# The second product of a two-layer product in threes: each output's three matmuls one after the other

## The chip, the cores and the metric

The kernel runs on one core of a Trainium2 chip. The metric is device time in microseconds of one execution; for the kernel before there are three runs and, apart from them, one execution under the hardware profiler, which gives the profile and the trace.

## What is computed

The reference first mixes a sequence in the frequency domain, then sends every token through two layers:

```python
X = np.fft.rfft(x, axis=1)                       # x: 8 x 3008 x 256
Yr = Xr @ w_r - Xi @ w_i + b_r
Yi = Xr @ w_i + Xi @ w_r + b_i
Yr = np.sign(Yr) * np.maximum(np.abs(Yr) - 0.01, 0.0)   # Yi in the same way
y = np.fft.irfft(Y, n=3008, axis=1)
h = np.maximum(y @ w_in, 0.0)                    # 24064 tokens, 256 -> 2048
out = (h * h) @ w_out                            # 2048 -> 256
```

## The kernel before

Matmuls with fp32 accuracy are made of three: an operand is split into a high part, its cast to F32R, and a low part, what the cast left of it. A product is then high x high + high x low + low x high, added up in PSUM. `mm3` (lines 179 to 184) issues these three for one output, one after the other: line 182 takes the first stationary part with the first moving part, line 183 the same stationary part with the second moving part, line 184 the second stationary part with the first moving part.

The transform is done in stages: A (a transform of 47 points, `plan_a`, tiles xin, f, fh, fl, psa), B (a transform of 64 points, the mix with the weights, the threshold and the way back, `plan_b`, tiles bin, psb, x, xh, xl, psm, e, z, zh, zl, psc) and D (the last transform back, `plan_d`, tiles din, psd, dv, dx). The stages hand over through scratch tensors in DRAM; all DMAs are issued by SyncE (SP). D writes the high and low parts xt of the token features for chunks of 512 tokens; there are 47 chunks.

The two layers run in rounds, eight per chunk, 376 in all and three more to empty the pipeline. In round r, TensorE (PE) does the following in this order, written out by hand at the end of the kernel:

- the first product of round r (`mm1`): 12 matmuls of 512 columns into ph, two banks of PSUM with no second buffer;
- what the plan puts at "p1": a stage's matmuls (psa, psb or psd);
- the block of the second product of round k = r - 3 (`mm2`): 21 matmuls of 256 columns into four banks po0 to po3, which collect over the eight rounds of a chunk;
- what the plan puts at "p2" (psm, psc, psa or psd).

The second product is a 2 x 2 scheme with seven products instead of eight: `PLACES` names for each of the seven the half of a bank that collects it, two in each of po0, po1 and po2 and one in po3. Its weights wo are the stationary operand and lie ready in a high part `wo_[0]` and a low part `wo_[1]`; its moving operand is the hidden layer, with high part gh and low part gl.

The other engines follow in each round. ScalarE (ACT): two times ReLU out of ph (line 876), the square (line 877), what the plan has at "e", then gh for round r - 1 (line 931), what the plan has at "f" and "a". VectorE (DVE): the sums that make the seven operands (lines 882 to 884), what the plan has at "e2", then gl for round r - 1 (line 936), and what the plan has at "f2" (the bias, lines 233 and 234, which reads psm) and "v". In the last round of a chunk `put_together` (lines 898 to 912) reads the four banks: one operation of ScalarE (line 902), seven of VectorE (lines 903 to 909); gh then comes after line 902, and gl after the seven and after "f" and "f2".

gh and gl have two buffers each. gh of round r - 1 is made in round r and read by the block of round r + 2. In round r its buffer was last in use by round r - 3, whose block runs in that same round r. So gh is written when the block of the same round has finished reading the buffer. Two more buffers matter: psa, psb, psd, psm and psc share two banks (`ps_f`), so that the next of them is written when VectorE or ScalarE has read the one before the last; and the banks po0 to po3 are single.

The block of the second product, before, first goes over the seven places with both weights and gh (line 891, 14 matmuls) and then over the seven places with the high weights and gl (line 895, 7 matmuls).

Of the kernel before, what the change touches and what calls it, by code (L numbers as in the profile page):

```python
# [130 lines left out]
PLACES = ((0, 0, 0), (2, 0, 1), (6, 1, 0), (5, 1, 1), (4, 2, 0), (3, 2, 1), (1, 3, 0))  # L131
NPR = 7
NU = NF // 2
# [3 lines left out]
HALF = CH // 2  # L137
# [12 lines left out]
def fft_mix_moe(ctx: ExitStack, tc: tile.TileContext, xp, xu, w_r, w_i, b_r, b_i,  # L150
                w_in, w_out, t_u, t_a, t_b, t_b0, t_m, t_d, sgn, outT):
    nc = tc.nc
# [19 lines left out]
    wo_ = [], []  # L172
# [6 lines left out]
    def mm3(out, lt, rt, start, stop, **kw):  # L179

        (l0, l1), (r0, r1) = lt, rt
        nc.tensor.matmul(out, l0, r0, start=start, stop=False, **kw)  # L182
        nc.tensor.matmul(out, l0, r1, start=False, stop=False, **kw)  # L183
        nc.tensor.matmul(out, l1, r0, start=False, stop=stop, **kw)  # L184
# [701 lines left out]
    def mm2(j, po, gh, gl):  # L886

        for s, bank, half in PLACES:
            out = po[bank][:, half * HALF:half * HALF + HALF]
            for k in range(2):  # L890
                nc.tensor.matmul(out, wo_[k][j][:, s], gh[:, s], start=j == 0 and half == 0 and k == 0,  # L891
                                 stop=False, skip_group_check=True)
        for s, bank, half in PLACES:
            out = po[bank][:, half * HALF:half * HALF + HALF]
            nc.tensor.matmul(out, wo_[0][j][:, s], gl[:, s], start=False, stop=j == NU - 1,  # L895
                             skip_group_check=True)

    def put_together(c, po):
        p = {s: po[bank][:, half * HALF:half * HALF + HALF] for s, bank, half in PLACES}
# [15 lines left out]
    with tc.manual_schedule():  # L915
        for r in range(last + LAG):
            c, j = divmod(r, NU)
# [6 lines left out]
            k = r - LAG  # L924
# [15 lines left out]
            if k >= 0:  # L940
                if jj == 0:
                    pos[cc] = [ps_o.tile([P, 512], F32, tag=f"o{i}", name=f"po{i}") for i in range(4)]
                mm2(jj, pos[cc], *split_.pop(k))
# [54 lines left out]
```

## Time and profile before

| | |
|---|---|
| three runs, us | 2605.96, 2604.91, 2600.55 (median 2604.91) |
| the profiled execution, us | 2602.41 |
| its span, us | 2600.6 |
| granted TensorE clock, mean | 0.992 |
| matmuls | 16496 |
| of them the second product | 5264 at line 891, 2632 at line 895 |
| gh (L931), count and mean ns | 376, 1697 |
| gl (L936), count and mean ns | 376, 2022 |

The span goes from the first to the last instruction. In the rows below, a group is one line of the program on one engine with its tiles: out<-in, shapes, count, then busy time in us and the mean of one in ns, then the idle time of the engine before it and what ended most of that. PEld is TensorE's loading of weights, which runs beside its matmuls (PE). A wait names who waited, for whom, how long in total, how often, and the longest. In the timeline a row has its start, its length, engine, line and operation; rows of equal instructions are merged, with their count. The chain is the work that ended last, followed back from the end.

### The profile page before, as it was taken

What the parts mean: (1) busy time and instruction counts of PE and PEld (TensorE: products, weight loads), DVE (VectorE), ACT (ScalarE), POOL (GpSimd) and SP (SyncE); (2) the same over time, 40 slices, a digit from 0 to 9 for tenths busy, and PEclk for the clock granted to TensorE, in tenths of its full rate; (3) what the DMA queues carried; (4) which work ended last, traced back from release to release, by engine and by line L of the source; (5) the groups of instructions that cost most, each with busy time, mean ns of one, the idle gap of its engine ahead of it and who ended that gap; (6) DMA issues with size and microseconds to landing.
All of it is one profiled execution on the core that took longest, in us unless ns stands there. A gap on an engine that the chain in (4) does not pass through costs nothing.

```text
span 2600.6 us, 41936 instructions
## 1 busy us (share of the span) xinstructions
PE 2540.9 (98%) x16496; PEld 2281.6 (88%) x16496; DVE 2106.6 (81%) x3155; ACT 1993.3 (77%) x2764; POOL 48.1 (2%) x57
## 2 busy tenths in 40 slices
PE   6979999999999999999999999999999999999999
PEld 3569999999999898999889998899989898999988
DVE  5868888888888888888888888788887888777776
ACT  3668887788788787778877887778777777777776
POOL 1410000000000000000000000000000000000000
PEclk8999999999999999999999999999999999999999
DMA  8621121212221112111122112121121111100000
GB/s 254 184 85 55 52 74 61 78 60 63 77 67 55 54 56 76 59 53 52 58 78 63 53 55 68 57 69 58 44 73 52 41 37 57 36 28 28 20 24 17
DMA packets 113094, 164.59 MB, mean 63 GB/s; under 512 B 9584, under 2 KB 63074, under 8 KB 112706
## 3 DMA queue, kind: packets, MB, share of 16 engines
q1 hardware_dynamic: 112898, 161.91, 19.8%
q8 instruction: 131, 2.15, 0.3%
q14 instruction: 65, 0.53, 0.1%
HBM read 86.90 MB, written 74.97 MB: 62 GB/s over the span
## 4 chain that ended last, share of the span: by engine, by line
PE 84%; DVE 7%; ACT 5%; DMA 2%; issue 1%; SPq 0%; DVEq 0%; ACTq 0%
PE po L891 21%; PE ph L182 12%; PE ph L184 12%; PE ph L183 12%; PE po L895 10%; PE psd L268 3%; PE psb L219 3%; PE psm L182 2%; PE psm L184 2%; PE psm L183 2%; DVE gl L936 2%; ACT g L876 1%; ACT g L877 1%; DMA din<-s 1%; DVE g L882 1%
## 5 line engine op out<-in xcount | busy, mean ns | idle before, releaser
L936 DVE TENSOR_TENSOR gl<-g,gh 128x1792 fp32r<-128x1792 f32 x376 | 760.3, 2022 | 32.2 <-ACT gh L931 23.2
L876 ACT ACTIVATE g<-ph 128x512 f32<-128x512 f32 x752 | 409.1, 596 | 458.0 <-PE ph L184 456.5
L891 PE MATMUL po<-gh,wo 128*128 128x256 f32 x5264 | 695.2, 282 | 1.6 <-DVE o L908 0.8
L891 PEld LDWEIGHTS po<-gh,wo 128*128 128x128 f32 x5264 | 651.8, 188 | 15.5 <-DVE o L908 4.6
L931 ACT CAST gh<-g 128x1792 fp32r<-128x1792 f32 x376 | 638.2, 1697 | 17.2 <-PE po L891 13.6
L182 PE MATMUL ph<-xt,wi 128*128 128x512 f32 x1504 | 593.1, 394 | 11.1 <-DVE dx L276 8.5
L184 PE MATMUL ph<-xt,wi 128*128 128x512 f32 x1504 | 590.8, 393 | 0.0
L183 PE MATMUL ph<-xt,wi 128*128 128x512 f32 x1504 | 589.3, 392 | 0.0
L882 DVE TENSOR_TENSOR g<-g 128x512 f32<-128x512 f32 x376 | 259.9, 691 | 330.5 <-ACT g L877 328.6
L877 ACT ACTIVATE g<-g 128x1024 f32<-128x1024 f32 x376 | 399.6, 1063 | 12.0
L895 PE MATMUL po<-gl,wo 128*128 128x256 f32 x2632 | 368.1, 279 | 0.0
L184 PEld LDWEIGHTS ph<-xt,wi 128*128 128x128 f32 x1504 | 282.9, 188 | 65.0
L182 PEld LDWEIGHTS ph<-xt,wi 128*128 128x128 f32 x1504 | 283.1, 188 | 63.6 <-ACT xt L280 8.7
L895 PEld LDWEIGHTS po<-gl,wo 128*128 128x128 f32 x2632 | 334.5, 188 | 0.0
L183 PEld LDWEIGHTS ph<-xt,wi 128*128 128x128 f32 x1504 | 283.2, 188 | 51.7
L884 DVE TENSOR_TENSOR g<-g 128x256 f32<-128x256 f32 x376 | 159.9, 425 | 12.9
L883 DVE TENSOR_TENSOR g<-g 128x256 f32<-128x256 f32 x376 | 159.8, 425 | 12.8
L182 PE MATMUL psm<-wm,xh 128*128 128x256 f32 (+1 forms) x552 | 163.1, 295 | 3.7 <-DVE dx L276 3.1
L184 PE MATMUL psm<-wm,xl 128*128 128x256 f32 (+1 forms) x552 | 161.2, 292 | 0.0
L183 PE MATMUL psm<-wm,xh 128*128 128x256 f32 (+1 forms) x552 | 160.6, 291 | 0.0
L219 PEld LDWEIGHTS psb<-tB,bin 128*128 128x128 f32 x768 | 101.1, 194 | 35.4 <-issue 17.4
L268 PEld LDWEIGHTS psd<-tD,din 120*128 120x128 f32 (+1 forms) x832 | 107.6, 191 | 18.1 <-DMA din<-s 7.2
(102 smaller groups left out, 2569.2 us busy)
## 6 DMA issues: line engine op xcount, KB each, us to landing
bin<-s SPq DMA_DIRECT2D x96, 256.0 KB
s<-evc SPq DMA_DIRECT2D x96, 256.0 KB
outT_dram<-o SPq DMA_DIRECT2D x94, 256.0 KB
din<-s SPq DMA_DIRECT2D x96, 240.0 KB
xin<-in_xp_dram SPq DMA_DIRECT2D x72, 240.0 KB
s<-eva SPq DMA_DIRECT2D x72, 240.0 KB
s<-eva SPq DMA_DIRECT2D x22, 192.0 KB
w<-in_moe_w_in_dram SPq DMA_DIRECT2D x8, 512.0 KB
```

The source lines that it names most:

```text
L182: nc.tensor.matmul(out, l0, r0, start=start, stop=False, **kw)
L183: nc.tensor.matmul(out, l0, r1, start=False, stop=False, **kw)
L184: nc.tensor.matmul(out, l1, r0, start=False, stop=stop, **kw)
L219: nc.tensor.matmul(ps[:, k, :, q, :], tv[:, q, k], tB[:, 0:r + 2:r + 1], start=True, stop=True)
L268: nc.tensor.matmul(ps[:, k, part], t[:n, s:s + P], tD[:n, tab + part, :n], start=True, stop=True)
L876: nc.scalar.activation(g[:, 2 * a:2 * a + 2], ph[:, a].rearrange("p (t m) -> p t m", t=2), AF.Relu)
L877: nc.scalar.activation(g[:, 0:4], g[:, 0:4], AF.Square)
L882: nc.vector.tensor_sub(g[:, 4:6], g[:, 1:4:2], g[:, 0:2])
L891: nc.tensor.matmul(out, wo_[k][j][:, s], gh[:, s], start=j == 0 and half == 0 and k == 0, stop=False, skip_group_check=True)
L895: nc.tensor.matmul(out, wo_[0][j][:, s], gl[:, s], start=False, stop=j == NU - 1, skip_group_check=True)
L931: nc.scalar.copy(split_[r - 1][0], hid[r - 1])
L936: nc.vector.tensor_sub(gl, hid.pop(r - 1), gh.bitcast(F32))
```

## The change

`mm2` issues the three matmuls of each place one after the other, by `mm3`, as the first product and the stages do already. The order of the places, the number of matmuls, their operands, the banks and the number of buffers of gh and gl stay as they are. `mm3` is given the high and low weights as its two stationary parts and gh and gl as its two moving parts; so the three are: high weights with gh, high weights with gl, low weights with gh.

```diff
     def mm2(j, po, gh, gl):
 
         for s, bank, half in PLACES:
-            out = po[bank][:, half * HALF:half * HALF + HALF]
-            for k in range(2):
-                nc.tensor.matmul(out, wo_[k][j][:, s], gh[:, s], start=j == 0 and half == 0 and k == 0,
-                                 stop=False, skip_group_check=True)
-        for s, bank, half in PLACES:
-            out = po[bank][:, half * HALF:half * HALF + HALF]
-            nc.tensor.matmul(out, wo_[0][j][:, s], gl[:, s], start=False, stop=j == NU - 1,
-                             skip_group_check=True)
+            mm3(po[bank][:, half * HALF:half * HALF + HALF], (wo_[0][j][:, s], wo_[1][j][:, s]),
+                (gh[:, s], gl[:, s]), j == 0 and half == 0, j == NU - 1, skip_group_check=True)
```

The lines behind it move up by six: gh is line 925 now, gl line 930, and `put_together`'s operations are lines 896 to 903.

## Prediction

> **What bounds the kernel now.** I read the page's busy times and its chain that ended last, then the main stretch alone, then the costliest groups and the waits, and last the timeline and the chain where a wait stands.
>
> ```profile
> span 2600.6 us, 41936 instructions
> PE 2540.9 (98%) x16496; PEld 2281.6 (88%) x16496; DVE 2106.6 (81%) x3155; ACT 1993.3 (77%) x2764; POOL 48.1 (2%) x57
> ...
> PE 84%; DVE 7%; ACT 5%; DMA 2%; issue 1%; SPq 0%; DVEq 0%; ACTq 0%
> ```
>
> TensorE is the bound: 98% busy, 84% of the chain. The same by stretch, for the rounds of the main loop (columns: stretch, its length, then busy time and instructions of PE, PEld, DVE, ACT, POOL, granted clock, DMA share, GB/s):
>
> ```profile
> 165.00:2595.00 2430.00, 2414.98 (x16040) 2202.66 (x16039) 2000.11 (x2981) 1908.13 (x2611) 0.00 (x0) 1.00 0.17 54
> ```
>
> PE stands for only 2430.00 - 2414.98 = 15 us of it, at a granted clock of 1.00. So no wait that goes can give much; the change gains only if matmuls come closer together, and loses wherever it makes PE wait. The groups of the second product, and the weight loads of one third of the first (which is in threes already):
>
> ```profile
> L891 PE MATMUL po<-gh,wo 128*128 128x256 f32 x5264 | 695.2, 282 | 1.6 <-DVE o L908 0.8
> ...
> L895 PE MATMUL po<-gl,wo 128*128 128x256 f32 x2632 | 368.1, 279 | 0.0
> ...
> L183 PEld LDWEIGHTS ph<-xt,wi 128*128 128x128 f32 x1504 | 283.2, 188 | 51.7
> ```
>
> And the waits of the main stretch (total, times, longest):
>
> ```profile
> ACT g L876 <- PE ph L184: 452.1, 264, 4.6
> ...
> ACT gh L931 <- PE po L891: 13.6, 21, 1.3
> ...
> PEld psb L219 <- DVE e L233: 10.5, 14, 1.2
> ...
> PE psb L219 <- DVE e L233: 5.3, 10, 0.8
> ...
> PEld po L891 <- DVE o L908: 4.6, 16, 0.5
> ```
>
> ScalarE mostly waits for PE (452 us before L876), but in 376 - 264 = 112 rounds it does not: there it has no slack. PE's own waits are for VectorE's read of the mix (L233), which frees the bank that the next psb writes.
>
> **The order of the matmuls.** PE, the end of the second product's block before a psc (po0 to po3 the four banks, gh and gl high and low operand, wo03 and wo13 high and low weights of one j). Before:
>
> ```order
> L891 MATMUL po2_12280<-gh_12348,wo13_909 128x256
> L891 MATMUL po3_12281<-gh_12348,wo03_908 128x256
> L891 MATMUL po3_12281<-gh_12348,wo13_909 128x256
> L895 MATMUL po0_12278<-gl_12349,wo03_908 128x256 x2
> L895 MATMUL po1_12279<-gl_12349,wo03_908 128x256 x2
> L895 MATMUL po2_12280<-gl_12349,wo03_908 128x256 x2
> L895 MATMUL po3_12281<-gl_12349,wo03_908 128x256
> L182 MATMUL psc_12511<-zh_12379,tMs_63 128x512
> ```
>
> The same place now:
>
> ```order
> L183 MATMUL po2_12280<-gl_12349,wo03_908 128x256
> L184 MATMUL po2_12280<-gh_12348,wo13_909 128x256
> L182 MATMUL po3_12281<-gh_12348,wo03_908 128x256
> L183 MATMUL po3_12281<-gl_12349,wo03_908 128x256
> L184 MATMUL po3_12281<-gh_12348,wo13_909 128x256
> L182 MATMUL psc_12511<-zh_12379,tMs_63 128x512
> ```
>
> The last reader of gh was the 14th of 21 matmuls and is now the 21st. The number of matmuls and loads is the same. What this costs in three places:
>
> **1. gh's buffer comes free seven matmuls later.** gh has two buffers and is written (L931) in the round in which the block that read the same buffer two rounds back runs. ScalarE is in order: what stands behind L931 waits with it. A place without slack, in the timeline, with the same place at its last occurrence behind it, and ScalarE's busy time between:
>
> ```profile
> 830.65 0.98 PE L895 MATMUL po<-gl,wo 128*128 128x256 f32 x7
> ...
> 830.87 1.70 ACT L931 CAST gh<-g 128x1792 fp32r<-128x1792 f32 x1
> ...
> 832.16 0.39 PE L182 MATMUL ph<-xt,wi 128*128 128x512 f32 x1
> ...
> 834.90 1.80 PE L891 MATMUL po<-gh,wo 128*128 128x256 f32 x14
> ...
> 836.09 1.08 ACT L876 ACTIVATE g<-ph 128x512 f32<-128x512 f32 x2
> ...
> 837.35 0.39 PE L182 MATMUL ph<-xt,wi 128*128 128x512 f32 x1
> ...
> 1922.67 1.08 ACT L876 ACTIVATE g<-ph 128x512 f32<-128x512 f32 x2
> ...
> 1923.93 0.39 PE L182 MATMUL ph<-xt,wi 128*128 128x512 f32 x1
> ```
>
> ```profile
> 830.90:837.10 6.20, 6.20 (x41) 5.59 (x40) 5.10 (x7) 6.15 (x11) 0.00 (x0) 1.00 0.27 85
> ```
>
> gh starts at 830.87, but the block ends at 830.65 + 0.98 = 831.63: gh moves by 0.76 and the hand-over, 0.8 us. ScalarE is busy for 6.15 of the 6.20 us that follow (evc, xh, four writes of z, fh), so L876 ends at 836.09 + 1.08 + 0.8 = 837.97. The next first product, which needs the banks that L876 empties, started at 837.35; it will wait some 0.6 us. I count 9 such places in the timeline, the first and last of them quoted: 9 x 0.6 = 5.5 us. Nothing waited there before.
>
> The other kind is on the chain already (start, length, piece; the first and the last of ten, one in full; then the block it should have waited for, from the timeline):
>
> ```profile
> 747.79 1.59 ACT gh L931
> ...
> 1232.15 1.70 ACT gh L931
> ...
> 1238.47 1.07 ACT g L877
> ...
> 1239.57 0.70 DVE g L882
> ...
> 1251.00 0.61 DVE e L233
> 1251.65 1.16 PE psb L219 x8
> ...
> 2190.51 1.70 ACT gh L931
> ```
>
> ```profile
> 1231.93 0.98 PE L895 MATMUL po<-gl,wo 128*128 128x256 f32 x7
> ```
>
> From gh at 1232.15 ScalarE, then VectorE carry the chain without a pause for 19 us, across a chunk's end with its eight operations, up to psb. The block ends at 1232.91: again 0.8 us, of which some 0.1 is lost in small gaps of the chain. 10 x 0.7 = 7 us. The rows behind gh on VectorE at that place, before:
>
> ```order
> L882 TENSOR_TENSOR g_12842<-g_12842 128x512 [waits Activation_49]
> L883 TENSOR_TENSOR g_12842<-g_12842 128x256 [waits DVE_49]
> L884 TENSOR_TENSOR g_12842<-g_12842 128x256 [waits DVE_49]
> L936 TENSOR_TENSOR gl_12857<-g_12765,gh_12856 128x1792 [waits PE_49,Activation_49]
> L233 TENSOR_TENSOR e_12908<-psm1_12884,bias2_68 128x512 [waits PE_49]
> ```
>
> and now (same order):
>
> ```order
> L882 TENSOR_TENSOR g_12842<-g_12842 128x512 [waits Activation_49]
> L883 TENSOR_TENSOR g_12842<-g_12842 128x256 [waits DVE_49]
> L884 TENSOR_TENSOR g_12842<-g_12842 128x256 [waits DVE_49]
> L930 TENSOR_TENSOR gl_12857<-g_12765,gh_12856 128x1792 [waits Activation_49]
> L233 TENSOR_TENSOR e_12908<-psm1_12884,bias2_68 128x512 [waits PE_49]
> ```
>
> gl no longer waits for PE itself, since gh has; L233 still stands behind it. Beside the ten there are up to 14 other waits of psb on L233 in the view of waits, whose push I can only bound by 0 and 0.8 us each; their gh starts mostly after part of the block is over, so I take 0.3: 4 us. In the other rounds ScalarE's 452 us of waiting cover the push. Loads and stores queue on SP behind evc, which moves with gh; I cost that at nothing, because din is asked for a round ahead; if it showed, each late din would cost up to 0.8 us.
>
> **2. gl is read at the second matmul, not the fifteenth.** In the loop it is a round early. At the end it is not:
>
> ```profile
> 2588.85 4.07 DVE L936 TENSOR_TENSOR gl<-g,gh 128x1792 fp32r<-128x1792 f32 x2
> 2588.90 0.98 PE L895 MATMUL po<-gl,wo 128*128 128x256 f32 x7
> 2589.14 1.71 ACT L931 CAST gh<-g 128x1792 fp32r<-128x1792 f32 x1 [0.36 <-PE po L891]
> ...
> 2592.17 1.80 PE L891 MATMUL po<-gh,wo 128*128 128x256 f32 x14
> ...
> 2594.23 0.37 ACT L902 COPY o<-po 128x256 f32<-128x256 f32 x1 [3.38 <-PE po L895]
> 2594.64 0.42 DVE L903 TENSOR_TENSOR o<-po,o 128x256 f32<-128x256 f32 x1 [1.73 <-ACT o L902]
> ```
>
> The last gh would start at 2588.90 + 0.98 = 2589.88 and end 1.71 later, the last gl 2.03 after that (half of 4.07), at 2593.7. The last block, begun at 2592.17, stands at its second matmul till then. Its first bank is whole after six matmuls and its second after twelve; with 0.117 us from one to the next (below) and 0.28 for the last to end, that is 2594.5 and 2595.2, against 2594.23 and 2594.64 now. VectorE's seven operations follow: 0.6 us.
>
> **3. The step from matmul to matmul.** The block at 834.90 has 21 in the 2.45 us up to 837.35, 0.1167 us each. The two other products in threes with the same width:
>
> ```profile
> 1242.29 0.28 PE L182 MATMUL psa<-fh,tAs 120*120 120x256 f32 x1
> ...
> 1243.00 2.14 PE L891 MATMUL po<-gh,wo 128*128 128x256 f32 x14
> ...
> 1245.79 0.28 PE L182 MATMUL psm<-wm,xh 128*128 128x256 f32 x1
> ...
> 1247.92 0.40 PE L182 MATMUL ph<-xt,wi 128*128 128x512 f32 x1
> ```
>
> Six psa take 0.71 us, 0.1183 each; eighteen psm take 2.13 us, 0.1183 each. If the order in threes does this, the 5264 + 2632 = 7896 matmuls cost 0.0016 us more each, 12 us; if the operands do it, nothing. Nothing in the trace tells them apart; both bounds stay in the range, and I take the middle, 6 us, since the operands are those of the quick rows and the order that of the slow ones. On the lower side stands a gain: half of ph's step, which is (834.90 - 832.16)/12 = 0.2283 us, is 0.1142, and 0.0025 x 7896 is 20 us less.
>
> The Trainium skill (TensorE: Matmul & The Clock Gate, "Part 2: What happens when you issue a matmul", the step on LDWEIGHTS) says that one loads a stationary operand once and multiplies with it repeatedly, which would speak for this change, since two of each three now share it. By that rule 2632 loads would go, and the sum could only fall. The row of L183 speaks against it: ph's second matmul shares its weights with the first, and still has 1504 loads for 1504 matmuls, of 188 ns.
>
> **What may come back.** The first block of a chunk waits for the reading of the third bank (L908, 4.6 us on PEld). That bank's first matmul is now the thirteenth, not the ninth, 4 x 0.117 = 0.47 us later, and the longest of these waits is 0.5. But VectorE reaches those reads later by the push above, and the first bank's by as much; I take 0 and keep 4.6 us as a gain for the range. The extra waits for PE that gl loses are no work of an engine.
>
> **Sum.** 5.5 + 7 + 4 + 0.6 + 6 = 23 us. The profiled execution took 2602.41 us (span 2600.6 and 1.8 around it), so 2625.4; the median of the runs, 2604.91, lies 2.5 us above it, so the same sum gives 2628 as the median.
>
> **The rivals.**
> *The push is absorbed.* gh comes later, but 264 of 376 rounds have a wait before L876 that takes it up, and 15 us of standing PE say that not much is tight. Then only the end's 0.6 us stays, less up to 4.6: 2601 to 2606. Against it: the ten places on the chain, where nothing can take it up.
> *It gets faster.* If two matmuls in a row with the same weights follow each other closer, by a load left out or in another way, the step falls towards 0.1142 us: 20 us less on PE. With the push kept that is 2628 - 6 - 20 = 2602; only if the push is absorbed too does it end on the other side, at 2585. It decides from a step below about 0.1145 us with the push kept. Against it: psa and psm in threes are slower, not quicker. The rule of the Trainium skill's page on TensorE named above would go this way.
> *The step alone decides.* The threes take 0.1183 us and PE, slower, gives ScalarE and VectorE 0.03 us more in each round, so that the push shrinks little: 17 + 12 = 29 us, 2634.
> *PE's stops feed on each other.* A stop at psb moves the next block and with it the next release of gh; if ScalarE has not caught up before the next tight place, pushes add. With 0.8 us at all 33 places (9, 10 and 14) and the slow step: 26.4 + 0.6 + 12 = 39 us, 2644.
>
> **How the numbers follow.** Median forecast 2628 with its own range: without the middle group and with the quick step 12.5 + 0.6 = 13 us (2618), with the slow step 2634. Chances: this forecast, with either step, 0.79; absorbed 0.13; faster 0.04; stops that add up 0.04. The range of 8 in 10 takes in the nearer half of the absorbed case through half-sized pushes (2608 = 2604.9 + 7 + 0.6 - 4.6) and, above, the slow step with pushes of full size at the 19 counted places and 0.4 at the rest (15.2 + 5.6 + 0.6 + 12 = 33): 2608 to 2638. Two runs of this kernel can be told apart from 0.2%, 5 us. Faster by more than that 0.05, within it 0.12, slower 0.83.
>
> **What would show it.** In the new profile gh's group should name PE's L184 (now the last matmul of the block) as what ended its idle time, far more often than 21 times and for 100 us or more in all; ACT's wait for ph should shrink; a wait of PE for L876 at ph should appear near nine places, and psb's waits for L233 should grow by 5 us or more. po's rows carry lines 182 to 184 with 2632 each; their step shows as the time from a block's first matmul to what follows it, 2.45 us now and 2.48 if the threes are slow. The prediction is wrong in its main step if gh waits and PE's idle time in the main stretch stays near 15 us; wrong in its third if blocks keep 2.45 us or fall below.

## The result, and the profile after

The kernel got slower: median 2621.79 us of three runs (2621.45 to 2624.29), against 2604.91 before; the ratio is 1.0072, interval 1.0049 to 1.0095. The profiled execution took 2621.79 us, 19.4 more than the one before.

The head of the page and the shares of the chain, after:

```profile
span 2619.9 us, 41621 instructions
...
PE 2543.8 (97%) x16496; PEld 2279.5 (87%) x16496; DVE 2109.6 (81%) x3155; ACT 2006.1 (77%) x2764; POOL 48.1 (2%) x57
...
PE 76%; DVE 8%; ACT 7%; issue 2%; DMA 1%; DVEq 0%; SPq 0%; ACTq 0%
```

Matmuls and loads are as many as before and PE is busy 3 us more, but its share of the chain fell from 84% to 76%. The main stretch (columns as before):

```profile
165.00:2615.00 2450.00, 2419.51 (x16027) 2201.01 (x16025) 2002.17 (x2981) 1919.74 (x2608) 0.00 (x0) 1.00 0.17 54
```

PE now stands 2450.00 - 2419.51 = 30.5 us instead of 15.0, at the same granted clock of 1.00. The groups of gh, gl and the second product (columns: busy, mean ns | idle before and what ended it):

```profile
L182 PE MATMUL po<-gh,wo 128*128 128x256 f32 x2632 | 751.1, 285 | 4.0 <-ACT xt L280 2.2 <-DVE o L898 1.8
L183 PE MATMUL po<-gl,wo 128*128 128x256 f32 x2632 | 734.2, 279 | 1.3 <-DVE gl L930 1.3
L184 PE MATMUL po<-gh,wo 128*128 128x256 f32 x2632 | 735.4, 279 | 0.0
...
L925 ACT CAST gh<-g 128x1792 fp32r<-128x1792 f32 x376 | 638.2, 1697 | 154.5 <-PE po L184 149.2
L930 DVE TENSOR_TENSOR gl<-g,gh 128x1792 fp32r<-128x1792 f32 x376 | 760.6, 2023 | 135.4 <-ACT gh L925 132.8
```

gh and gl take as long as before, but ScalarE stands 149.2 us before gh for the block's last matmul. Two waits of ScalarE and the waits of PE:

```profile
ACT g L876 <- PE ph L184: 347.2, 221, 4.3
...
ACT gh L925 <- PE po L184: 149.2, 247, 2.1
```

```profile
PE psb L219 <- DVE e L233: 11.0, 14, 1.3
PE ph L182 <- ACT g L876: 4.4, 9, 0.5
PE psm L182 <- DVE dx L276: 3.9, 4, 1.2
PE psd L268 <- DMA din<-s: 3.3, 5, 1.3
PE po L182 <- ACT xt L280: 2.2, 5, 0.6
PE po L182 <- DVE o L898: 1.8, 5, 0.9
PE po L183 <- DVE gl L930: 1.3, 1, 1.3
```

gh waits 247 times, before 21 times and 13.6 us. ScalarE's wait for ph fell from 452.1 to 347.2: about 105 of the 136 us were absorbed there. What was not absorbed reaches PE, at ph (no such row before) and at psb.

**One place of each kind.** At ph, the place that stood at 830.65 to 837.35 before:

```profile
833.86 0.28 PE L184 MATMUL po<-gh,wo 128*128 128x256 f32 x1
834.18 1.70 ACT L925 CAST gh<-g 128x1792 fp32r<-128x1792 f32 x1 [0.70 <-PE po L184]
...
839.39 1.08 ACT L876 ACTIVATE g<-ph 128x512 f32<-128x512 f32 x2
...
840.52 0.50 PE L182 MATMUL ph<-xt,wi 128*128 128x512 f32 x1 [0.49 <-ACT g L876]
```

gh starts after the block's last matmul, L876 ends at 839.39 + 1.08 = 840.47, and ph, which followed the block 2.45 us after its start before, starts at 840.52, 3.11 us after the block's first matmul:

```profile
837.41 0.28 PE L182 MATMUL po<-gh,wo 128*128 128x256 f32 x1
```

At psb, the place whose gh started at 1232.15 before; first before, then after:

```profile
1232.74 0.40 PE L182 MATMUL psc<-zh,tMs 128*128 128x512 f32 x1
```

```profile
1241.20 0.40 PE L182 MATMUL psc<-zh,tMs 128*128 128x512 f32 x1
1241.40 1.70 ACT L925 CAST gh<-g 128x1792 fp32r<-128x1792 f32 x1 [0.69 <-PE po L184]
...
1251.41 0.42 DVE L898 TENSOR_TENSOR o<-po,o 128x256 f32<-128x256 f32 x1
...
1251.98 0.36 PE L182 MATMUL po<-gh,wo 128*128 128x256 f32 x1 [0.36 <-ACT xt L280]
...
1260.89 0.49 PE L219 MATMUL psb<-tB,bin 128*128 128x128 f32 x2 [1.26 <-DVE e L233]
```

From psc, which follows the block, to psb it was 1251.65 - 1232.74 = 18.91 us and is 1260.89 - 1241.20 = 19.69: 0.78 more. Two thirds of that came at 1251.98 already, where the chunk's first block waits for its first bank, which is read behind gh too: that block began 1243.00 - 1232.74 = 10.26 us after psc, and now begins 10.78 after. The row names ScalarE's L280, which ended last before it, but what the block waited for is VectorE's L898, the last read of the first bank: at all ten places of this kind the block starts 0.15 us after L898 has ended, whichever of the two the row names. Within the block 0.20 us come back, since its wait for the third bank is gone, and 0.46 more are lost at psb.

**Where the 19.3 us of the span lie.** PE's matmuls fall into 1229 stretches of one tile, in the same order in both traces; the time from each stretch's first matmul to the next one's, after minus before, gives: nine places of the first kind 5.9 us (0.65 each), ten of the second 7.8 (0.78 each), the rest of the loop 8.5, the six chunk ends of the last 300 us -2.1, so 20.1 for the loop; 0.8 at the end; -1.6 before 165 us. A second profile of the changed kernel (below) has -0.04 there, so that part is scatter.

### The profile page after: what moved, and what is told of

It reads as the page before. It is cut to its first block, busy times and chain, and to the rows that moved or that the text cites. A ratio compares the mean times of both kernels' runs of the same rounds, so it can differ in the third digit from the quotient of the medians.

```text
span 2619.9 us, 41621 instructions
## 1 busy us (share of the span) xinstructions
PE 2543.8 (97%) x16496; PEld 2279.5 (87%) x16496; DVE 2109.6 (81%) x3155; ACT 2006.1 (77%) x2764; POOL 48.1 (2%) x57
## 4 chain that ended last, share of the span: by engine, by line
PE 76%; DVE 8%; ACT 7%; issue 2%; DMA 1%; DVEq 0%; SPq 0%; ACTq 0%
PE ph L182 11%; PE ph L184 11%; PE ph L183 10%; PE po L182 10%; PE po L184 10%; PE po L183 10%; PE psb L219 3%; PE psd L268 3%; DVE gl L930 2%; PE psm L182 2%; PE psm L184 2%; PE psm L183 2%; ACT g L876 2%; ACT z L740 1%; ACT g L877 1%
## 5 line engine op out<-in xcount | busy, mean ns | idle before, releaser
L930 DVE TENSOR_TENSOR gl<-g,gh 128x1792 fp32r<-128x1792 f32 x376 | 760.6, 2023 | 135.4 <-ACT gh L925 132.8
L925 ACT CAST gh<-g 128x1792 fp32r<-128x1792 f32 x376 | 638.2, 1697 | 154.5 <-PE po L184 149.2
L182 PE MATMUL po<-gh,wo 128*128 128x256 f32 x2632 | 751.1, 285 | 4.0 <-ACT xt L280 2.2
L183 PE MATMUL po<-gl,wo 128*128 128x256 f32 x2632 | 734.2, 279 | 1.3 <-DVE gl L930 1.3
L184 PE MATMUL po<-gh,wo 128*128 128x256 f32 x2632 | 735.4, 279 | 0.0
L876 ACT ACTIVATE g<-ph 128x512 f32<-128x512 f32 x752 | 408.4, 595 | 353.0 <-PE ph L184 351.4
L184 PE MATMUL ph<-xt,wi 128*128 128x512 f32 x1504 | 590.4, 393 | 0.0
L183 PE MATMUL ph<-xt,wi 128*128 128x512 f32 x1504 | 589.3, 392 | 0.0
L182 PEld LDWEIGHTS po<-gh,wo 128*128 128x128 f32 x2632 | 495.3, 188 | 12.2 <-ACT xt L280 3.5
L183 PEld LDWEIGHTS po<-gl,wo 128*128 128x128 f32 x2632 | 495.2, 188 | 6.3 <-DVE gl L930 1.5
L184 PEld LDWEIGHTS po<-gh,wo 128*128 128x128 f32 x2632 | 494.9, 188 | 0.0
L184 PEld LDWEIGHTS ph<-xt,wi 128*128 128x128 f32 x1504 | 282.8, 188 | 64.8
L183 PEld LDWEIGHTS ph<-xt,wi 128*128 128x128 f32 x1504 | 283.0, 188 | 51.6
L184 PE MATMUL psm<-wm,xl 128*128 128x256 f32 (+1 forms) x552 | 160.6, 291 | 0.0
L183 PE MATMUL psm<-wm,xh 128*128 128x256 f32 (+1 forms) x552 | 160.0, 290 | 0.0
```

Of the source, the lines that this page charges most:

```text
L876: nc.scalar.activation(g[:, 2 * a:2 * a + 2], ph[:, a].rearrange("p (t m) -> p t m", t=2), AF.Relu)
L925: nc.scalar.copy(split_[r - 1][0], hid[r - 1])
L930: nc.vector.tensor_sub(gl, hid.pop(r - 1), gh.bitcast(F32))
```

## The experiments

The runs were made in groups, each with its own runs of the kernel before beside it: 2602.05 us is their median in the first group, 2601.74 in the second.

The theory: gh's buffer comes free later, because its last reader is now the block's last matmul, and what stands behind gh on ScalarE and VectorE comes later with it. The rivals: the order in threes itself costs something on PE (the step), or gl, read at the second matmul, is the wait that counts.

**One matmul moved, no threes.** The order before, but its 14th matmul, the last that reads gh, comes last (in the second variant 18th):

```diff
-        for s, bank, half in PLACES:
...
+        order = [(k, s, bank, half) for s, bank, half in PLACES for k in range(2)]
+        order[-1:] = [(2, *p) for p in PLACES[:7]] + order[-1:] + [(2, *p) for p in PLACES[7:]]
+        for i, (k, s, bank, half) in enumerate(order):
...
+                             (gl if k == 2 else gh)[:, s], start=j == 0 and half == 0 and k == 0,
```

(In the second variant 4 stands for 7.)

> The order of before, with one of its 21 matmuls moved: the 14th, the last that reads gh, goes to the end of the block, behind the seven that read gl. No threes; gl is read from the 14th matmul on. Theory of the late release (gh's buffer comes free 0.8 us later and pushes ScalarE, VectorE and then PE): nearly the whole loss of the changed kernel, +13 to +19 us against before, with gh waiting for PE some 240 times for 150 us, and waits of PE for L876 before ph at nine places. Rival, the threes themselves (the step from matmul to matmul, or the weights): 0, within 3 us of before. Rival, gl read early in the block: 0, within 3 us.

> The order of before, with the last matmul that reads gh moved from the 14th to the 18th place: the release comes 4 x 0.117 = 0.47 us later instead of 0.82. Theory of the late release: each push is 0.35 us smaller, so ten places x 0.35 + nine x 0.27 + about 1 for the rest = +7 us against before (4 to 10). Rivals (threes, early gl): 0. If the loss were one of any late release, whatever its size, it would be near +15.

Measured: as the last 2624.41 us against 2602.05, ratio 1.0089 (1.0076 to 1.0103); as the 18th 2611.83, ratio 1.0040 (1.0026 to 1.0053). One matmul at the block's end costs all that the change costs, without any threes: 22.4 us, more than the 13 to 19 expected. The 18th place costs 9.8 us, within the 4 to 10 expected. The profiled execution of the first variant took 5597 us, so nothing is read from its trace, and the kernel was run again, unedited:

> The kernel with one matmul of gh at the end of the block once more, on the same chip as the changed kernel, for its trace. Theory of the late release: +19 to +24 us against before; the stops of PE stand at the same places as the changed kernel's, and what it has beyond the changed kernel (2 to 5 us) are the waits for the third bank at a chunk's first block, which the threes take away and this order doesn't. Rival: a difference spread evenly over the blocks (a step from matmul to matmul).

Measured: 2625.94 against 2601.74, ratio 1.0091 (1.0078 to 1.0105), 24.2 us. Its main stretch and waits:

```profile
165.00:2615.00 2450.00, 2422.14 (x16021) 2200.93 (x16020) 2001.91 (x2982) 1920.15 (x2611) 0.00 (x0) 1.00 0.17 54
```

```profile
ACT g L876 <- PE ph L184: 347.2, 222, 4.2
...
ACT gh L929 <- PE po L891: 156.9, 249, 2.2
...
PEld po L891 <- DVE o L906: 6.3, 16, 0.5
...
PE ph L182 <- ACT g L876: 4.4, 9, 0.5
```

The same 347.2 us, the same nine stops at ph. By stretches the loop lost 22.7 us: the nine places 5.9, the ten 7.8, as in the changed kernel. Beyond the two profiles of the changed kernel it has 2.6 and 4.7 us: 2.1 at the six chunk ends, where the wait for the third bank (L906 here), which the changed kernel lost, is still there, and for the rest mostly psd's waits for its load. In the 18th-place variant:

```profile
ACT g L876 <- PE ph L184: 410.9, 240, 4.5
...
ACT gh L929 <- PE po L891: 75.4, 165, 1.8
...
PEld ph L182 <- ACT g L876: 3.1, 9, 0.4
```

The loop lost 8.1 us: the nine places 2.7, the ten 4.05. So a release four matmuls later (4 x 0.1167 = 0.47 us) costs 0.30 and 0.41 a place, seven later (0.82 us) 0.65 and 0.78: in both variants the delay less 0.17 at ph and less 0.04 to 0.06 at psb, which can be read as the slack that these places had.

**Threes, with gh free early.** The changed kernel, but the last three of the seven places read gl wherever they read gh, so that gh is last read at the 12th matmul and a part of the product is missing:

```diff
-        for s, bank, half in PLACES:
-            mm3(po[bank][:, half * HALF:half * HALF + HALF], (wo_[0][j][:, s], wo_[1][j][:, s]),
-                (gh[:, s], gl[:, s]), j == 0 and half == 0, j == NU - 1, skip_group_check=True)
+        for n, (s, bank, half) in enumerate(PLACES):
+            mm3(po[bank][:, half * HALF:half * HALF + HALF], (wo_[0][j][:, s], wo_[1][j][:, s]),
+                ((gh if n < 4 else gl)[:, s], gl[:, s]), j == 0 and half == 0, j == NU - 1, skip_group_check=True)
```

> The changed kernel in threes, but the last three of the seven places read gl where they should read gh, so that part of the product is left wrong; the number, shapes and order of the matmuls stay. gh is last read at the 12th matmul instead of the 21st, gl still at the second. Theory of the late release: the loss is gone, 2597 to 2606 us (the end's 0.6 us stays, the waits for the third bank at a chunk's first block fall by up to 4.6 us). Rivals: the threes cost time by their order, or gl read at the second matmul does: 2615 to 2624 us, as the changed kernel.

Measured: 2600.45, ratio 0.9994 (0.9985 to 1.0003). The threes, their sharing of weights and the early reading of gl are all kept, and nothing is lost: both rivals fall. Its blocks of 21 take 2.45 us as before. Its waits and main stretch:

```profile
ACT g L876 <- PE ph L184: 454.3, 267, 4.6
...
PE psb L219 <- DVE e L233: 8.7, 10, 1.3
ACT gh L925 <- PE po L184: 7.5, 13, 1.1
```

```profile
165.00:2590.00 2425.00, 2407.22 (x16007) 2198.88 (x16008) 1996.92 (x2977) 1900.04 (x2606) 0.00 (x0) 1.00 0.17 54
```

One row needs care: psb waits 8.7 us for L233, before 5.3, with no time lost. By stretches PE reaches the p2 work behind a chunk's first block 3.45 us earlier in all, since the wait for the third bank is gone, and then stands 3.36 us longer at the next psb: ten places, 0.35 us each. VectorE sets the end there, and PE's gain is handed back. Only where no psb follows, at the six chunk ends of the last 300 us, is it kept: 2.1 us, as in the changed kernel.

**A release earlier than before.** The order before, the last two places' first two matmuls reading gl, so that gh is last read at the 10th instead of the 14th and a part of the product is missing:

```diff
-                nc.tensor.matmul(out, wo_[k][j][:, s], gh[:, s], start=j == 0 and half == 0 and k == 0,
+                nc.tensor.matmul(out, wo_[k][j][:, s], (gl if s in (3, 1) else gh)[:, s], start=j == 0 and half == 0 and k == 0,
```

> The order of before, but the last two places read gl instead of gh in their first two matmuls, so that part of the product is left wrong: gh is last read at the 10th matmul instead of the 14th, a release 0.47 us earlier than before. Theory of the late release: before has next to no loss left from it, since ScalarE itself is late at the ten places on the chain: 0 to -2 us against before. Rival, that the time follows the release in both directions: -7 us, as the 18th place costs +8 to +10.

Measured: 2602.51 against 2601.74, ratio 1.0001 (0.9992 to 1.0010); the loop -0.1 us.

```profile
ACT gh L931 <- PE po L891: 5.2, 9, 0.8
```

The wait before gh falls from 13.6 to 5.2 us and the time does not follow, where 0 to 2 us less was expected and 7 less by the rival: the 14th place was early enough.

**Threes only in a chunk's first round.** The order before in seven rounds of eight, threes in the round that follows the reading of the banks:

```diff
     def mm2(j, po, gh, gl):
 
+        if j == 0:
+            for s, bank, half in PLACES:
+                mm3(po[bank][:, half * HALF:half * HALF + HALF], (wo_[0][j][:, s], wo_[1][j][:, s]),
+                    (gh[:, s], gl[:, s]), half == 0, False, skip_group_check=True)
+            return
```

> The order of before in seven of a chunk's eight rounds, the threes only in the first, where the third bank's first matmul then comes 0.47 us later. Theory of the late release: a late gh in that round is not on the chain (VectorE is behind by its end-of-chunk work then), so the loss of the threes does not come, and the waits for the bank's reading go: -2 to -4 us against before (ratio 0.9985 to 0.9992). Rival, that every late release costs: an eighth of the changed kernel's loss, +2 us, less the same gain, near 0.

Measured: 2599.53, ratio 0.9990 (0.9981 to 0.9998). Its waits:

```profile
PEld psb L219 <- DVE e L233: 13.8, 14, 1.7
...
ACT gh L936 <- PE po L184: 16.6, 34, 0.9
ACT gh L936 <- PE po L896: 14.6, 21, 1.3
```

The wait for the third bank is gone. The late release stays in one round of eight, where gh waits 34 times (L184), and nothing is lost by it: at the nine places and the ten the time is as before. The six chunk ends keep their 2.1 us. With the whole product it is the quickest order here, 2.5 us or 0.1% below before; the interval ends just under 1.

**The changed kernel again, and psm's order.** The changed kernel unedited, and with psm's three matmuls in the order that takes both operands with the high weights first:

> The changed kernel, not edited, beside the one before it on the same chip: 1.006 to 1.008 against before, and 2 to 5 us below the kernel with one matmul last.

> The changed kernel, with the mix's three matmuls (psm) in another order: high operand with high weights, low operand with high weights, high operand with low weights, so that two in a row share the moving operand and not the stationary one. It is about the step alone. If sharing the stationary operand sets the step of 0.1183 us of psm, a block of 18 takes 2.10 us instead of 2.13 (0.1167 each). If the operands or the place set it, it stays at 2.13. The whole time should not move by more than 3 us in either case.

```diff
-                    mm3(p[bank][:, half * D:half * D + D], (s["h"][:, comp, k], s["l"][:, comp, k]),
-                        (wm[0][:, mat, k], wm[1][:, mat, k]), k == 0, k == 1)
...
+                    nc.tensor.matmul(out, h, w0, start=k == 0, stop=False)
+                    nc.tensor.matmul(out, l, w0, start=False, stop=False)
+                    nc.tensor.matmul(out, h, w1, start=False, stop=k == 1)
```

Measured: the first 2621.80 against 2601.74, ratio 1.0077 (1.0063 to 1.0091), the loop +18.1 us with 5.9 and 7.8 in the two kinds of places; it differs from the first profile mostly in the waits of psd for its load (PE's 3.3 us are 1.7 there). The second was run once, 2624.05 beside 2604.84: psm's stretches of 18 take 2130 ns, in the changed kernel 2129. So the order does not make psm's step of 0.1183 us; whether its operands or its place do stays open.

A third buffer for gh, with which its next write would no longer wait for this block, was not tried.

## Why the prediction was right, and where its sizes were off

- **Verdict and mechanism: right.** 16.9 us were lost by the medians first taken and 20.1 by those of the repeat, 23 were forecast. The release of gh is shown as the cause from both sides: alone it costs the whole loss, and without it the threes cost nothing.
- **Step 1, ph:** nine places at 0.6, 5.5 us; measured nine at 0.65, 5.9.
- **Step 1, the ten places on the chain:** 7 forecast, 7.8 measured. The small gaps of the chain took up 0.04 us, not 0.1. The forecast put all of it on psb; 5.2 us arrive already at the chunk's first block, which now waits for the reading of its first bank; 2.3 of them come back within that block, and 4.9 are lost at psb.
- **Step 1, the rest:** 4 us forecast, from up to 14 other waits of psb; measured 6.5 and 8.5 in two profiles. The bound was good and the place was not: only some five other psb were later, 1.6 us together, and 3.1 us fell on nine rounds in which psm stands between the block and the first product, which the forecast did not count. The other 1.9 to 3.8 us are differences of under 0.15 us each and the loads of psd, in which the two profiles differ from each other.
- **Step 2, the end:** 0.6 forecast, 0.8 measured. The wait for gl (L930, 1.3 us) fell on the last block but one, not on the last: of the two gl that were written back to back before, the first now ends the wait.
- **Step 3, the step from matmul to matmul: this term was mis-sized.** "I take the middle, 6" between 0 and 12; it is 0. Blocks of 21 followed by a first product take 2.453 us before and 2.454 now, in the median of 186; by the prediction's own sign ("wrong in its third if blocks keep 2.45 us") this step was wrong. A middle between two exclusive causes was the value that neither of them could give. Without it the sum is 17 us, against 16.9 and 20.1 by the medians and 19.4 and 18.9 by the two profiled executions. That the total came as near as it did is in part luck: the rest of step 1, too small by 2.5 to 4.5 us, hid part of the 6.
- **What may come back, taken as 0:** 2.1 us came back, where the forecast had not looked, at the chunk ends without a psb behind them; at the other ten, VectorE took it as argued.
- **The rivals.** *Absorbed*: 105 of 136 us were, the rest was enough. But the 112 rounds that the prediction calls without slack, since ScalarE does not wait before L876, were not all tight: PE came over 0.1 us later at some 40 places only. *Faster*: two of each three matmuls share their weights, and still there are 2632 loads at L183 for 2632 matmuls, of 188 ns, as the row of ph had said. The Trainium skill (TensorE: Matmul & The Clock Gate, "Part 2: What happens when you issue a matmul") says that a stationary operand can be loaded once and multiplied with repeatedly; no load was saved in this way here:

```profile
L183 PEld LDWEIGHTS po<-gl,wo 128*128 128x128 f32 x2632 | 495.2, 188 | 6.3 <-DVE gl L930 1.5
```

- *Stops that feed on each other*: of the 19 counted places 18 lost less than the delay of 0.82 us. One of the ten (psb at 1727.1 before) lost 0.96, in both profiles and with one matmul last too. VectorE's last read of the banks begins 0.54 us after the one before it there, and 0.33 in the other 46 chunks and in all 47 before; why is not shown.
- **One of the tests was weaker than it looked.** "psb's waits for L233 should grow by 5 us or more": they did, from 5.3 to 11.0, but 3.4 of the 5.7 also appear in the kernel that loses nothing, and with one matmul last, which loses as much, PE's wait there is 6.2 us. A wait that grows shows a loss only if what lies ahead of it did not get shorter.

## What to carry to other kernels

A buffer is free after its last reader, so an order of matmuls is also an order of releases: finish first with the operand whose writer stands in front of other work on an engine that works in order. Look for the rounds without slack, since there a delay counts almost in full (0.65 to 0.78 of 0.82 us here) while the sum of all waits shows that most of it vanishes; and before taking a middle value, ask whether the two ends exclude each other. Reordering for the sake of one wait pays only where nothing else ends later: the wait for the third bank was worth 0.35 us at six places and nothing at ten.

## What the runs showed of the hardware that was not expected

The spacing of the matmuls did not depend on their order here: 0.1167 us in a block with the same weights in two neighbours and without, and psm's 0.1183 in both of its orders. And a row's idle time on PE can grow by almost two thirds (psb in the kernel with gh free early, 5.3 to 8.7 us) while the kernel's time does not change. The engine that a row names as the end of a wait need not be the one that ended it: five of the ten waits for the first bank are put down to ScalarE's L280 (2.2 us), and all ten end 0.15 us after VectorE's L898.
